# Linear attention and a gated feed-forward layer on one core: the late sums of g behind the fourth division, and the units of seven products in block 2 too

## The chip, the cores and the metric

One core of a Trainium2 chip runs the kernel. The metric is the device time of one execution in microseconds. Before the change it is 277.55 us, the median of three runs (277.35 to 277.58).

## The reference

The inputs are q, k and v of shape [8, 8, 576, 64] (batch, heads, positions, head width), w_in [512, 2048] and w_out [2048, 512], all float32. The first stage is linear attention with position weights, the second a feed-forward layer:

```
phi(x) = concat(relu(x) * cos_w, relu(x) * sin_w)      # features 64 -> 128, weights by position
kv  = sum over s of phi(k)[s, f] * v[s, d]             # per batch and head, 128 x 64
z   = sum over s of phi(k)[s, f]
x   = (phi(q) @ kv) / (phi(q) @ z + 1e-6)              # heads side by side: [4608, 512]
h   = x @ w_in
g   = h * sigmoid(1.702 * h)
out = g @ w_out                                        # [4608, 512] float32
```

## The kernel before

One block of work is one batch, 576 rows of x: four chunks of 128 rows and a chunk of 64. The 512 rows are multiplied with w_in and w_out in the block; the 64-row chunks of all batches are collected in `xt` and worked off in the last block. Matrix operands are bf16, sums float32 in PSUM.

**What a block does.** While block b is multiplied, the x of block nb = b + 1 is made. For nb, feature maps of k (`trig`, two VectorE instructions for each of nine column groups) go to `kr`; `kv_next` multiplies them with v (72 small matmuls at L237) and VectorE copies the result out (L245). Then `x_next(nb, c)` (L965) makes chunk c of x in three steps: `num_mm` (L304), eight matmuls of 65 columns into a PSUM tile of the pool `pat`; `num_div` (L315), three VectorE instructions (L321 adds 1e-6, L323 inverts, L325 multiplies and writes bf16); `xturn_dma` (L351), a transposing DMA from SP's queue into the tile xT. The pool `pat` has two tiles, so the numerator of chunk c + 2 waits for the division of chunk c.

**The product with w_out** uses Winograd's form of Strassen's scheme: seven products of half size in place of eight. They are called p1, p2, p6, p5, p7, p3, p4, in this order (L481), each in two halves of eight matmuls of 256 columns (`wino_mm`, L509). Steps s = 0 to 13 of the loop at L1021 are these fourteen halves. The operands that are sums of blocks of g are made by `g_sums` (L466) on VectorE, each in two halves h of 1024 columns: s1 and s2 (read by p5 and p6), s3 (read by p7) and s4 (read by p3). Results go from three PSUM banks through copies on ScalarE (`keep`, L528: p1, u2, p5) and sums on VectorE (`join`, L539) to `ysb`, and out by DMAs that GpSimd issues (L526).

**The product with w_in** has two forms. In the plain form (`mm1`, L373) it is sixteen column groups fc of four matmuls of 512 columns (L365), each followed by the gelu on ScalarE (L371). In the form with units (`mm1_pair`, L724) two objects of class `Unit` (L643) make eight of the sixteen groups with seven products of half size each (L658, 256 columns), and the other eight go the plain way (`mm1_at`, L718, into `pat`, and L768, L773). A unit needs sums of blocks of w_in (`win_sum`, L615, held in `ws_pair` inside the tile `gt`), sums of blocks of x (`x_pair`, L712, made at the end of the block before), three VectorE adds (L667) and three ScalarE copies (L672), for which seven slots in `gt` and in the three `kept` tiles serve in rotation (L708). Blocks in PAIR (L699), 3 to 6, take the form with units; blocks 0, 1 and 2 the plain one; block 7 takes another with four units.

**What sets the order.** The kernel is scheduled by hand: each engine works off its instructions in the order in which the program states them, and waits at each one for the semaphores of its operands. The loop at L971 states it for a block. In the wino loop, a step states its products, then the keep or join of the product that has ended, then `x_next` for the chunks in `at` (L1017), then a feature map of the block after next's q on ScalarE (`trig_q`, from step 4 on in blocks 3 to 5, from step 8 on in blocks 1 and 2) with its transposing DMA on SP (`qturn_dma`), and then `g_sums`. In blocks 3 to 6 `x_next` of chunk 0 stands ahead of step 0 and the others at steps 1, 3, 4 and 6 (in block 6 the chunks 4, 1, 2, 3); `g_sums` of s3 stand at step 1 and of s4 at step 5. Block 2 has the divisions at steps 1, 3, 5 and 7 and makes s3 and the first half of s4 earlier, at fc 12. SP's queue carries the loads of q, k and v and all transposes, in the order of the program: the load of v for the block after next behind chunk 3 (L1030), then chunk 4's transpose, the five of q, then in the next block the loads of q and k (L749, in `mm1_pair` behind the last feature map of k; L986 in the plain form).

**Block 0** is a start-up with its own order. VectorE's part of it that the change touches is L915 to L921: after the fifth division it makes the eighteen feature maps of block 1's k (from the load at L844), then the first sum of w_out's blocks (`w_sum_1`). The block of w_in that holds its last 1024 columns is loaded at L843. The sums of w_in for the units are made in block 2 (L992).

Of the kernel before, what the change touches and what calls it, by code (L numbers as in the profile page):

```python
# [20 lines left out]
def kernel(  # L21
# [9 lines left out]
    nc = tc.nc  # L31
    B, H, S, D = q.shape
# [24 lines left out]
    def src_of(src, b, i0=0, i1=NI):  # L57
        return src[b, 2 * i0:2 * i1].rearrange("(i hh) (p j) d -> (hh p) i (j d)", hh=2, j=NS)

    qf = one.tile([128, 2560], F32, name="qf")  # L60
    kf, vf = [one.tile([128, NI, S], F32, name=n) for n in ("kf", "vf")]
# [62 lines left out]
    def load(t, src, b, eng=nc.gpsimd):  # L124
        eng.dma_start(out=t, in_=src_of(src, b))
# [24 lines left out]
    def load_wout(g):  # L150
        nc.gpsimd.dma_start(out=w_out_sb[:, ts(g, 4), :], in_=wout_r[g])
# [9 lines left out]
    def trig(dst, src, j, act=False, eng=nc.vector):  # L161

        i = src[:, :, ts(j, 64)]
        for cs, w in enumerate((cosw, sinw)):
            o = dst[:, j, :, ts(cs, 64)]
            if act is True or (act == "sin" and cs == 1):
                nc.scalar.activation(o, i, AF.Relu, scale=w[:, j:j + 1])
            else:
                eng.tensor_scalar(o, i, 0.0, w[:, j:j + 1], op0=MAX, op1=MUL)  # L169
# [73 lines left out]
    def kv_evac(i0, i1, n=65):  # L243
        o = st["kvs"][:, :, i0:i1, 0:n]
        nc.vector.tensor_copy(o, st["ps", i0].rearrange("p hh (i e) -> p hh i e", e=n))  # L245
# [58 lines left out]
    def num_mm(c, eps_too=False):  # L304
        ps = pat.tile([128, 2, 512], F32, name="at")
        if eps_too:
            for a in range(2):
                put_eps(ps[:, a])
        for h in range(H):
            nc.tensor.matmul(ps[:, h // 4, ds((h % 4) * 65, 65)], qT[:, h, ts(c, 128)],  # L310
                             kvs_of(h), start=not eps_too,
                             stop=(not eps_too or h % 4 == 3), skip_group_check=eps_too)
        nums[c] = [ps]

    def num_div(c, eps_too=False):  # L315
        ps = nums[c][0]
        pv = ps[:, :, 0:260].rearrange("p a (h e) -> p a h e", h=4)
        den = pv[:, :, :, 64]
        if not eps_too:
            den = small.tile([128, 2, 4], F32, name="den")  # L320
            nc.vector.tensor_scalar(den, pv[:, :, :, 64], 1e-6, None, op0=ADD)  # L321
        inv = small.tile([128, 2, 4], F32, name="inv")
        nc.vector.reciprocal(inv, den)  # L323
        xn = small.tile([128, 2, 4, 64], BF16, name="xn", bufs=5)
        nc.vector.tensor_tensor(xn, pv[:, :, :, 0:64],  # L325
                                inv.unsqueeze(3).to_broadcast([128, 2, 4, 64]), op=MUL)
        nums[c].append(xn)
# [23 lines left out]
    def xturn_dma(b, c):  # L351
        xn = nums.pop(c)[1]
        n = 128 if c < 4 else 64
        nc.sync.dma_start_transpose(out=x_cols(b, c),
                                    in_=xn[0:n].rearrange("p a h e -> p (a h e)"))
# [110 lines left out]
    def g_sums(names, h, of=MAIN):  # L466

        tt = nc.vector.tensor_tensor
        a_blk, to = of
        o = {n: to[n][:, ts(h, 4)] for n in to}  # L470
        for n in names:
            if n == "s1":
                tt(o[n], a_blk(1, h), a_blk(1, h + 2), op=ADD)  # L473
            elif n == "s2":
                tt(o[n], o["s1"], a_blk(0, h), op=SUB)  # L475
            elif n == "s3":
                tt(o[n], a_blk(0, h), a_blk(1, h), op=SUB)  # L477
            else:
                tt(o[n], a_blk(0, h + 2), o["s2"], op=SUB)
# [135 lines left out]
    def win_sum(n, i, ws=ws):  # L615
        tt = nc.vector.tensor_tensor
        o = {m: ws[m][:, :, ts(i, 512)] for m in ws}
        a = {(0, k): w_in_t[i][:, ts(k, 2), :] for k in range(2)}
        a.update({(1, k): w_in_t[2][:, ts(k, 2), ts(i, 512)] for k in range(2)})
        if n == "s1":  # L620
            tt(o[n], a[1, 0], a[1, 1], op=ADD)
        elif n == "s2":
            tt(o[n], o["s1"], a[0, 0], op=SUB)
        elif n == "s3":
            tt(o[n], a[0, 0], a[1, 0], op=SUB)
        else:
            tt(o[n], a[0, 1], o["s2"], op=SUB)
# [15 lines left out]
    class Unit:  # L643
# [31 lines left out]
        def step(self, p):  # L675
# [17 lines left out]
            else:  # L693
# [2 lines left out]

    PAIR = range(3, B - 1)  # L699
    gt_flat = gt.rearrange("p f e -> p (f e)")  # L700
    ws_pair = {n: gt_flat[:, ts(i, 1024)].rearrange("p (k f) -> p k f", k=2)
               for i, n in enumerate(("s1", "s2", "s3", "s4"))}
# [86 lines left out]
    def kv_mm_next():  # L789
        kv_open()  # L790
        kv_mm(0, 4, vt_rhs, 0, 65)

    def kv_next():
        kv_mm_next()
        kv_evac(0, 4)
# [120 lines left out]
    load_wout(2)  # L916
    load(vf, v, 1)
    load_wout(3)
    for j in range(NS):
        trig(kr, kf, j)  # L920
    w_sum_1()  # L921
# [43 lines left out]
    def x_next(b, c):  # L965
        num_mm(c)
        num_div(c)
        xturn_dma(b, c)


    for b in range(1, B):  # L971
        nb = b + 1 if b + 1 < B else None
        if nb is None:
            break
        f0 = 5 if b == 1 else 0
        if b in PAIR:
            mm1_pair(b, nb)
        for fc in range(f0, FC) if b not in PAIR else ():
            if b == 1 and fc == f0:
                for c in range(5):  # L980
                    trig_q(c)
                    qturn_dma(c)
            if nb is not None and fc == f0 + 1:
                kv_operands(nb)

                if nb + 1 < B:  # L986
                    if b == 1:
                        load(kf, k, nb + 1, nc.sync)
                    load_q(nb + 1, nc.sync)
                    if b > 1:  # L990
                        load(kf, k, nb + 1, nc.sync)
                if b == 2:  # L992
                    for n in ws_pair:
                        win_sum(n, 0, ws_pair)
            if fc == 8 and b == 1:
                vcopy()
            if fc == 12:
                if b > 1:
                    g_sums(("s3",), 0)
                    g_sums(("s3",), 1)  # L1000
                g_sums(("s1", "s2", "s4") if b > 1 else ("s1", "s2"), 0)
            if fc == 14 and nb is not None and b > 1:
                kv_next()
            mm1(b, fc)
        if nb is not None:
            x_open(nb)
            if b == 2:
                x_next(nb, 0)
            if b == 1:
                kv_mm_next()  # L1010
            g_sums(("s1", "s2"), 1)
            if b > 2:
                x_next(nb, 0)
            if b == 1:
                kv_evac(0, 4)
                g_sums(("s3",), 0)
            at = ({2: [0], 3: [1], 4: [2], 6: [3], 8: [4]} if b == 1 else  # L1017
                  {2 * p + 1: [p + 1] for p in range(4)} if b == 2 else
                  {s: [p + 1 if nb < B - 1 else (4, 1, 2, 3)[p]] for p, s in enumerate((1, 3, 4, 6))})
            wino_open()  # L1020
            for p in range(7):  # L1021
                for c in range(2):
                    wino_mm(p, c)
                    s = 2 * p + c
                    if c == 1:
                        wino_after(b, p)
                    for c2 in at.get(s, ()):
                        x_next(nb, c2)
                        if c2 == 3 and nb + 1 < B:
                            load(vf, v, nb + 1, nc.sync)  # L1030

                    s0 = 4 if b > 2 else 8
                    if s0 <= s < s0 + 5 and nb + 1 < B:
                        trig_q(s - s0, act=True)
                    if 8 <= s < 13 and nb + 1 < B:
                        qturn_dma(s - 8)
                    if s == 1 and b == 2:
                        g_sums(("s4",), 1)
                    if s == 1 and b > 2:
                        g_sums(("s3",), 0)  # L1040
                        g_sums(("s3",), 1)
                    if s == 5 and b > 2:
                        g_sums(("s4",), 0)
                        g_sums(("s4",), 1)
                    if s == 2 and b == 1:
                        g_sums(("s3",), 1)
                    if s == 4 and b == 1:
                        g_sums(("s4",), 0)
                    if s == 6 and b == 1:
                        g_sums(("s4",), 1)  # L1050
            if nb in PAIR:
                x_pair(nb)
# [3 lines left out]
    b = B - 1  # L1056
# [103 lines left out]
```

## Time and profile before

| what | value |
|---|---|
| median of three runs | 277.55 us |
| the profiled execution | 277.53 us, span 275.6 us |
| TensorE (PE) busy | 267.9 us, 97% of the span |
| VectorE (DVE) busy | 203.0 us, 74% |
| ScalarE (ACT) busy | 172.8 us, 63% |
| GpSimd (POOL) busy | 43.0 us, 16% |
| blocks 2, 3, 4, 5, 6 by the chain of waits | 28.60, 28.50, 28.49, 28.48, 28.49 us |
| granted TensorE clock | 1.00 |
| HBM | 36.70 MB read, 9.44 MB written |

The span runs from the program's first instruction to its last; the execution's own time holds 1.9 us more around it. A group's busy time counts overlapping instructions once. A matmul's drawn length covers its way through the array, so matmuls that follow each other overlap in the record: what one costs is the distance of its start to the next start (0.109 us for 256 columns, 0.216 us for 512). VectorE's and ScalarE's instructions overlap a little in the same way: a product L325 is drawn 0.69 us long and the next instruction starts after 0.61. A bracket behind an instruction holds the idle time of its engine just before it and what ended it.

### The profile page before, as it was taken

To read this page: it belongs to the slowest core of one execution; us is meant where nothing else is said; L and a number is where in the kernel's file an instruction comes from. 1 tells how busy PE (TensorE), PEld (TensorE's weight loads), DVE (VectorE), ACT (ScalarE), POOL (GpSimd) and SP (SyncE) were. 2 spreads that over 40 slices of the span, in tenths; PEclk is the share of its full clock that TensorE was granted. 3 is DMA by queue.
4 is the path that set the end of the run, shared out by engine and by line. 5 is a ranking of instruction groups with operands and counts; after the bars stand their busy time and mean duration, and the time that the engine had idled before them with its cause. 6 is when DMAs were issued, how large, how long until landed. Compare 5 with 4: busy or idle time off the path is not lost.

```text
span 275.6 us, 6999 instructions
## 1 busy us (share of the span) xinstructions
PE 267.9 (97%) x2844; PEld 204.5 (74%) x2844; DVE 203.0 (74%) x476; ACT 172.8 (63%) x311; POOL 43.0 (16%) x71
## 2 busy tenths in 40 slices
PE   8899999999999999999999999999999999999994
PEld 2585645856975699778877887788778876999983
DVE  4943775698899596879887988888888985744741
ACT  6967642584297519974788387848683147677621
POOL 5691000000122012100210022001200163000310
PEclk9999999999999999999999999999999999999999
DMA  7999999999999897997799689999991754000233
GB/s 232 253 211 298 278 295 162 255 305 197 301 207 289 225 262 192 255 242 206 187 299 233 195 114 278 170 284 194 236 196 23 107 149 139 0 0 2 82 111 114
DMA packets 73663, 53.60 MB, mean 194 GB/s; under 512 B 52736, under 2 KB 63488, under 8 KB 73632
## 3 DMA queue, kind: packets, MB, share of 16 engines
q1 hardware_dynamic: 67504, 36.97, 60.9%
q0 software_dynamic: 6128, 16.19, 22.6%
q8 instruction: 22, 0.36, 0.6%
q14 instruction: 9, 0.07, 0.1%
HBM read 36.70 MB, written 9.44 MB: 167 GB/s over the span
## 4 chain that ended last, share of the span: by engine, by line
PE 81%; DVE 12%; DMA 4%; issue 1%; ACT 0%; POOL 0%
PE mm L520 22%; PE mm L365 16%; PE mm L658 14%; PE at L721 8%; PE mm L421 5%; PE at L520 4%; PE mm L396 4%; PE at L237 4%; DVE xn L325 3%; DMA sums<-in_v_dram 2%; DVE sums L475 2%; PE at L310 2%; DVE sums L477 2%; DVE sums L473 2%; DMA kf<-in_k_dram 1%; DVE inv L323 1%
## 5 line engine op out<-in xcount | busy, mean ns | idle before, releaser
L365 PE MATMUL mm<-xT,w_in 128*128 128x512 bf16 (+1 forms) x304 | 51.4, 320 | 0.0
L526 POOL DMA_DIRECT2D out_dram<-ysb x24 | 18.1, 754 | 182.0 <-DVE den L321 124.6
L520 PEld LDWEIGHTS <-sums 128*128 128x128 bf16 x448 | 42.5, 98 | 4.6
L371 ACT ACTIVATE g<-mm 128x512 bf16<-128x512 f32 x56 | 32.2, 597 | 14.6 <-PE mm L365 14.6
L365 PEld LDWEIGHTS <-w_in 128*128 128x128 bf16 x304 | 27.6, 114 | 17.3
L520 PE MATMUL mm<-wsum,sums 128*128 128x256 bf16 x336 | 39.9, 272 | 0.0
L520 PEld LDWEIGHTS <-g 128*128 128x128 bf16 x336 | 32.0, 98 | 3.6
L169 DVE TENSOR_SCALAR kr<-kf,cosw 128x256 bf16<-128x256 f32 x69 | 24.5, 355 | 5.3 <-DMA kf<-in_k_dram 5.3
L325 DVE TENSOR_TENSOR xn<-at,inv 128x512 bf16<-128x512 f32 x39 | 27.0, 691 | 1.3
L520 PE MATMUL mm<-w_out_sb,g 128*128 128x256 bf16 x224 | 26.6, 273 | 0.0
L169 DVE TENSOR_SCALAR kr<-kf,sinw 128x256 bf16<-128x256 f32 x68 | 23.5, 345 | 0.0
L721 PE MATMUL at<-xT,w_in 128*128 128x512 bf16 x96 | 23.3, 379 | 0.0
L183 ACT ACTIVATE qn<-qf,cosw 128x512 bf16<-128x512 f32 (+1 forms) x27 | 19.2, 712 | 2.2 <-DMA qf<-in_q_dram 2.2
L183 ACT ACTIVATE qn<-qf,sinw 128x512 bf16<-128x512 f32 (+1 forms) x27 | 19.2, 710 | 0.0
L535 ACT ACTIVATE kept_p<-mm 128x512 f32<-128x512 f32 (+1 forms) x15 | 8.5, 566 | 16.7 <-PE mm L520 14.9
L658 PE MATMUL mm<-xT,w_in 128*128 128x256 bf16 x128 | 18.6, 273 | 0.0
L658 PEld LDWEIGHTS <-w_in 128*128 128x128 bf16 x144 | 15.9, 113 | 2.7
L310 PEld LDWEIGHTS <-qT 128*128 128x128 bf16 x312 | 13.8, 97 | 5.1 <-issue 3.7
L658 PE MATMUL mm<-xT,gt 128*128 128x256 bf16 x128 | 17.2, 272 | 0.0
L310 PE MATMUL at<-kvs,qT 128*128 128x65 bf16 x312 | 15.7, 193 | 1.3 <-DVE den L321 1.3
L535 ACT ACTIVATE kept_u<-mm 128x512 f32<-128x512 f32 (+1 forms) x8 | 4.4, 544 | 18.8 <-PE mm L520 15.4
L658 PEld LDWEIGHTS <-gt 128*128 128x128 bf16 x128 | 14.1, 113 | 2.4 <-issue 0.9
(175 smaller groups left out, 452.6 us busy)
## 6 DMA issues: line engine op xcount, KB each, us to landing
kf<-in_k_dram SPq DMA_DIRECT2D x6, 1152.0 KB, 9.1
vf<-in_v_dram SPq DMA_DIRECT2D x6, 1152.0 KB, 7.0
qf<-in_q_dram SPq DMA_DIRECT2D x6, 1024.0 KB, 6.5
out_dram<-ysb POOLq DMA_DIRECT2D x24, 256.0 KB, 5.5
w_out_sb<-in_moe_w_out_dram POOLq DMA_DIRECT2D x4, 512.0 KB, 17.2
kf<-in_k_dram POOLq DMA_DIRECT2D x1, 1152.0 KB, 13.1
vf<-in_v_dram POOLq DMA_DIRECT2D x1, 1152.0 KB, 20.3
w_in<-in_moe_w_in_dram POOLq DMA_DIRECT2D x2, 512.0 KB, 10.0
```

Source lines behind the costliest of these rows:

```text
L169: eng.tensor_scalar(o, i, 0.0, w[:, j:j + 1], op0=MAX, op1=MUL)
L183: nc.scalar.activation(o, i, AF.Relu, scale=sc)
L310: nc.tensor.matmul(ps[:, h // 4, ds((h % 4) * 65, 65)], qT[:, h, ts(c, 128)], kvs_of(h), start=not eps_too, stop=(not eps_too or h % 4 == ...
L325: nc.vector.tensor_tensor(xn, pv[:, :, :, 0:64], inv.unsqueeze(3).to_broadcast([128, 2, 4, 64]), op=MUL)
L365: nc.tensor.matmul(hp[fc][:, t0:t1], wcol(kc, fc), x[b][:, kc, t0:t1], start=(kc == 0), stop=(kc == KC - 1))
L371: nc.scalar.activation(gT[fc // 4][:, fc % 4], hp.pop(fc), AF.Gelu_apprx_sigmoid)
L421: nc.tensor.matmul(yp[b, t, c0][:, c0:c1], w, w_out_sb[:, fc, c0:c1], start=(fc == 0), stop=(fc == FC - 1))
L520: nc.tensor.matmul(bank[to][c], lhs, rhs, start=opens, stop=(fc == HF - 1), skip_group_check=True)
L526: eng.dma_start(out=dst[:, 2 * i + c0:2 * i + c1, ts(n, HD)], in_=t[:, c0:c1])
L535: nc.scalar.activation(o, i, AF.Identity)
L658: nc.tensor.matmul(to[:, j], lhs, rhs, start=(opens and j == 0 and k == 0), stop=(k == 1), skip_group_check=True)
L721: nc.tensor.matmul(hp[fc], wcol(kc, fc), x[b][:, kc], start=(kc == 0), stop=(kc == KC - 1))
```

## The change

`PAIR` begins at block 2, so that block 2 takes the form with units as well (and `x_pair` for it runs at the end of block 1). The four sums of w_in's blocks that it needs are made in block 0, ahead of the feature maps of block 1's k. What block 2 did otherwise than blocks 3 to 6 in its own loop goes away: its divisions now stand at steps 1, 3, 4 and 6 too, and chunk 0's behind the second halves of s1 and s2; its feature maps of q stay at steps 8 to 12. In blocks 2 to 6 the four halves of s3 and s4 all stand at step 4, behind `x_next` of that step, which is the fourth division of the block.

```diff
-    PAIR = range(3, B - 1)
+    PAIR = range(2, B - 1)
...
     load(vf, v, 1)
     load_wout(3)
+    for n in ws_pair:
+        win_sum(n, 0, ws_pair)
     for j in range(NS):
         trig(kr, kf, j)
     w_sum_1()
...
                 if nb + 1 < B:
-                    if b == 1:
-                        load(kf, k, nb + 1, nc.sync)
+                    load(kf, k, nb + 1, nc.sync)
                     load_q(nb + 1, nc.sync)
-                    if b > 1:
-                        load(kf, k, nb + 1, nc.sync)
-                if b == 2:
-                    for n in ws_pair:
-                        win_sum(n, 0, ws_pair)
             if fc == 8 and b == 1:
                 vcopy()
             if fc == 12:
-                if b > 1:
-                    g_sums(("s3",), 0)
-                    g_sums(("s3",), 1)
-                g_sums(("s1", "s2", "s4") if b > 1 else ("s1", "s2"), 0)
-            if fc == 14 and nb is not None and b > 1:
-                kv_next()
+                g_sums(("s1", "s2"), 0)
             mm1(b, fc)
         if nb is not None:
             x_open(nb)
-            if b == 2:
-                x_next(nb, 0)
             if b == 1:
                 kv_mm_next()
             g_sums(("s1", "s2"), 1)
-            if b > 2:
+            if b > 1:
                 x_next(nb, 0)
...
             at = ({2: [0], 3: [1], 4: [2], 6: [3], 8: [4]} if b == 1 else
-                  {2 * p + 1: [p + 1] for p in range(4)} if b == 2 else
                   {s: [p + 1 if nb < B - 1 else (4, 1, 2, 3)[p]] for p, s in enumerate((1, 3, 4, 6))})
...
-                    if s == 1 and b == 2:
-                        g_sums(("s4",), 1)
-                    if s == 1 and b > 2:
-                        g_sums(("s3",), 0)
-                        g_sums(("s3",), 1)
-                    if s == 5 and b > 2:
-                        g_sums(("s4",), 0)
-                        g_sums(("s4",), 1)
+                    if s == 4 and b > 1:
+                        for n in ("s3", "s4"):
+                            g_sums((n,), 0)
+                            g_sums((n,), 1)
```

## The prediction

> **What bounds the kernel now.** I read the page's engine shares and its chain first, then the busy time of each engine over the blocks, then VectorE's and TensorE's instructions in order of time inside one block.
>
> ```profile
> PE 267.9 (97%) x2844; PEld 204.5 (74%) x2844; DVE 203.0 (74%) x476; ACT 172.8 (63%) x311; POOL 43.0 (16%) x71
> ...
> PE 81%; DVE 12%; DMA 4%; issue 1%; ACT 0%; POOL 0%
> ```
>
> TensorE is the bound, yet 12% of the chain that ends last is VectorE's. The chain shows where the blocks start, at 80.68, 109.28, 137.78, 166.27, 194.75 and 223.24 us. The windows between them are blocks 2 to 6; here blocks 2, 3 and 4 (columns: window, its length, busy us of PE, PEld, DVE, ACT, POOL, clock, DMA):
>
> ```profile
> 80.68:109.28 28.60, 28.60 (x291) 20.50 (x289) 21.58 (x50) 17.87 (x31) 3.61 (x5) 1.00 0.98 245
> 109.28:137.78 28.50, 28.18 (x315) 22.84 (x313) 24.04 (x58) 21.11 (x39) 2.91 (x5) 1.00 0.89 224
> 137.78:166.27 28.49, 28.17 (x314) 22.82 (x313) 24.03 (x58) 20.32 (x36) 2.90 (x5) 1.00 0.91 214
> ```
>
> Block 2 multiplies w_in in the plain way and never idles. Blocks 3 to 6 already use the two units of seven products, and save only 0.1 us by it: each has the same hole. In block 4 the chain goes through it:
>
> ```profile
> 156.69 1.28 DVE sums L477 x2
> 157.97 0.60 DVE ysb L545
> ...
> 158.91 0.69 DVE xn L325
> 159.61 0.08 DVE den L321
> 159.69 0.06 issue
> 159.75 0.40 PE at L310 x8
> ```
>
> The same place in VectorE's and TensorE's order of time:
>
> ```profile
> 156.08 0.69 DVE L325 TENSOR_TENSOR xn<-at,inv 128x512 bf16<-128x512 f32 x1
> 156.69 1.28 DVE L477 TENSOR_TENSOR sums<-g 128x1024 bf16<-128x1024 bf16 x2
> 157.89 0.68 DVE L545 TENSOR_TENSOR ysb<-mm,kept_p 128x512 f32<-128x512 f32 x1
> 158.49 0.16 DVE L321 TENSOR_SCALAR den<-at 128x8 f32<-128x8 f32 x1
> ...
> 159.52 0.16 DVE L321 TENSOR_SCALAR den<-at 128x8 f32<-128x8 f32 x1
> ...
> 160.56 1.28 DVE L479 TENSOR_TENSOR sums<-g,sums 128x1024 bf16<-128x1024 bf16 x2
> ```
>
> ```profile
> 157.53 1.91 PE L520 MATMUL mm<-wsum,sums 128*128 128x256 bf16 x16
> 159.75 0.40 PE L310 MATMUL at<-kvs,qT 128*128 128x65 bf16 x8 [0.32 <-DVE den L321]
> ```
>
> The fifth numerator (chunk 4, at 159.75) needs the PSUM tile of the third (chunk 2), which is free when the third division's product ends (158.91 + 0.69 = 159.60; then 0.15 to TensorE). That division stands behind the two s3 sums. How large is the hole? The sixteen matmuls issue every 0.109 us (157.53, 157.635, ..., 159.16), so the numerator could start at 159.27: 0.48 us. The bracket says 0.32, because the last matmul is drawn 0.27 long. The Trainium skill ("Perfetto Trace Analysis", Identifying the Most-Contended Engine) warns that matmul busy time is a poor measure because pipelined matmuls look different from what they cost; with 0.32 in the sum below it would end at 276.1. The spacing decides: 0.48.
>
> **The change part by part** (times of the profiled execution, 277.53 us with a span of 275.6; the median of the runs shown is 277.55, so one sum serves for both).
>
> 1. *Late sums, blocks 3 to 6.* New order on VectorE: divisions 1 and 2, the join of p1 and p2 (L545), divisions 3 and 4, s3 twice, s4 twice, division 5. Up to 156.69 nothing moves. Then: join 0.60 to 157.29; third division 1.03 (158.49 to 159.52) to 158.32, its product written at 158.40, plus 0.15 is 158.55. TensorE asks at 159.27, so the 0.48 goes, with 0.72 to spare. What is late next: fourth division to 159.35, s3 twice at 0.60 to 160.55, s4 twice to 161.75, fifth division to 162.78 (before: 162.80). The seventh product p7 reads s3. TensorE is there at 159.27 + 0.24 (numerator) + 0.87 (eight matmuls of p5) = 160.39 and needs the second half four matmuls later, 160.82; that half is written at 160.63 and reaches TensorE at 160.78. Cover 0.04 us, the thinnest of all. p3 reads s4: first matmul at 160.39 + 1.75 = 162.13, halves with TensorE at 161.38 and 161.98; the second is needed at 162.57. Free. The join of p7 then runs at 162.78 to 163.38 and p4 writes that bank at 163.88. Free.
>
>  p3 also writes the bank that ScalarE's copy of p5 reads:
>
> ```profile
> 160.93 0.71 ACT L183 ACTIVATE qn<-qf,sinw 128x512 bf16<-128x512 f32 x1
> 161.54 0.58 ACT L535 ACTIVATE kept_p<-mm 128x512 f32<-128x512 f32 x1
> ```
>
>  The copy queues behind four feature maps of q, does not move, and ends at 162.12; with the 0.15 to TensorE p3 starts at 162.27 at the latest instead of 162.13. Bounds: 0 (copy seen at once) to 0.14; I take 0.10. Block 6 has no feature maps of q, so nothing there. Gain: blocks 3, 4, 5 each 0.48 - 0.10 = 0.38, block 6 0.48; together **1.62**.
>
> 2. *Units in block 2.* Leaves: 64 matmuls of 512 columns at 0.216 = 13.82. Comes: 32 x 0.216 + 56 x 0.109 = 13.02, so 0.80 less TensorE work. What comes with it (six adds, six copies, four x sums, the waits of the units' banks) need not be priced singly: blocks 3 to 6 hold all of it. Block 2 becomes a block of 28.49 with the hole, 28.01 without: 28.60 - 28.01 = **0.59**. Its copy of p5 is ahead of its feature maps of q (they stay at steps 8 to 12), so the 0.10 does not arise. Late at its start: the x sums wait for the fourth chunk of block 2's x, whose DMA is issued at 76.27 and lands 4.25 later, 80.52. Four sums take 1.46 (108.18 to 109.64 in block 3), six feature maps of k 1.57: 83.55. The first add cannot start before block start + 3.31 (112.43 - 109.12) = 80.56 + 3.31 = 83.87. Covered by 0.3. ScalarE enters block 2 at 82.29 + 0.48, some 0.3 later against its start than in block 3; the first bank that this can hold up is the third regular product's, with about 0.1 to spare. Between 0 and 0.2 lost; I take 0, as in block 3. SP's loads of q and k stand behind five transposes until 91.35 in both kernels, and the k feature maps end before (88.5), so they do not move.
>
> 3. *w_in sums in block 0.* Four sums at 0.63 (86.26 to 88.79 for four) = 2.53 leave block 2 and come ahead of block 1's feature maps of k. VectorE idles there:
>
> ```profile
> 26.74 0.35 DVE L169 TENSOR_SCALAR kr<-kf,cosw 128x256 bf16<-128x256 f32 x1 [2.68 <-DMA kf<-in_k_dram]
> ```
>
>  It is free at 24.06, the last third of w_in lands at 12.81 + 11.1 = 23.91, and 24.06 + 2.53 = 26.59 is ahead of 26.74. Cost 0. Without that cover the feature maps slip, by at most 2.53, and a second idle time of 2.2 us (35.05, for q) takes it.
>
> Sum: 1.62 + 0.59 = 2.21. **277.53 - 2.21 = 275.3 us.** With p3's wait at 0 or 0.14, the units' start at 0 to 0.2: 275.0 to 275.6.
>
> **The rivals.**
>
> *The wait moves.* p7 has 0.04 of cover. If the four sums go at 0.69 each, as where one sum waits for another (L475), and not 0.60, s3's second half comes 0.18 later and p7 stalls 0.14 in five blocks: 276.0. For it: the cover is thin. Against: s3 and s4 read nothing that was just written, and ran at 0.60 in pairs.
>
> *The transfers do not follow.* The feature maps of q of block 5 start late, at 184.80, held 1.28 us by the load of q: 18.7 us after the block's start (166.10), against 14.9 for that load in block 4. ScalarE then needs 1.24 + 0.49 + 2.45 + 0.58 + 0.1 until p5's copy is done, so p3 (24.5 after the start) stalls from a landing at 19.6. If the transfers keep their old clock while TensorE gains 1.35 us by block 5, the load lands at 20.05: 0.4 lost, 275.8 with its neighbours. [...] Against: an earlier load also ends earlier.
>
> *Slower.* The same queue, further: between blocks 4 and 5 one slow stretch cost the load of q 3.8 us. A second such stretch ahead of block 5 would bring it at 18.7 + 0.4 + 3.8 = 22.9 and p3 would stall 3.3: 278.6. It decides from a landing 2.8 us past 19.6. Against: one stretch in four blocks, and the next load is issued only after the last.
>
> *The sums' move does nothing*, since the numerator waits for something else than the third product. Then block 2 alone counts, 28.60 to 28.49: 277.4. Against: the wait ends 0.15 after that product in all four blocks.
>
> **How the numbers follow.** Forecast 0.62 (275.0 to 275.6), the moved wait 0.15 (276.0), transfers 0.10 (275.8), nothing moved 0.07 (277.4), slower 0.06 (278.6). The range 274.8 to 276.6 holds the first three with a margin for their bounds. A measurement of this kernel tells 0.2%, 0.55 us, from no change: faster 0.87, same 0.07, slower 0.06.
>
> **What would show it.** Blocks 2 to 6 about 28.0 to 28.1 long; no idle time ahead of the fifth numerator; VectorE's four sums in a row, ending near block start + 24.1; p3's first matmul behind the copy of p5 by 0.1 in blocks 3 to 5; the w_in sums between 24.06 and 26.7 with the feature maps of k starting where they did. Wrong would be a new gap ahead of p7, a block 2 longer than its fellows, or ScalarE waiting for q in blocks 4 and 5 by several us.

## The result, and the profile after

The changed kernel takes **275.37 us** (median of 6 runs, 275.05 to 276.1) against 277.52 for the kernel before (6 runs beside it): a ratio of 0.9926, 95% interval 0.9913 to 0.994. It is faster by 2.15 us; the forecast was 275.3. Executions in which TensorE's granted clock was lowered are left out of all figures: there were three, all of the changed kernel in a second set (mean clock 0.85, 0.85 and 0.56; 309, 309 and 461 us).

The page of the changed kernel; its profiled execution took 275.49 us around a span of 273.4:

```profile
PE 265.7 (97%) x2847; PEld 207.2 (76%) x2868; DVE 207.8 (76%) x487; ACT 174.8 (64%) x317; POOL 42.4 (15%) x71
...
PE 93%; DMA 4%; DVE 1%; issue 1%; ACT 0%; POOL 0%
```

VectorE has more to do than before (207.8 us instead of 203.0) and is hardly on the chain any more: its part of it falls from 12% to 1%, TensorE's rises from 81% to 93%. An engine's share of busy time says nothing about whether it is waited for. Blocks 2, 3, 5 and 6 of the changed kernel (block 4 has 28.05; columns: window, its length, busy us of PE, PEld, DVE, ACT, POOL, clock, DMA):

```profile
80.82:108.84 28.02, 27.86 (x311) 22.92 (x313) 24.91 (x60) 20.00 (x37) 2.90 (x5) 1.00 1.00 247
108.84:136.88 28.04, 27.88 (x311) 22.88 (x313) 23.95 (x58) 21.20 (x39) 2.90 (x5) 1.00 1.04 245
...
164.93:193.04 28.11, 27.95 (x312) 22.90 (x313) 23.96 (x58) 20.31 (x36) 2.91 (x5) 1.00 0.93 224
193.04:221.06 28.02, 27.86 (x311) 22.84 (x312) 24.03 (x57) 14.31 (x26) 2.93 (x5) 1.00 0.61 131
```

The lengths were 28.60, 28.50, 28.49, 28.48 and 28.49: the five blocks give back 0.58, 0.46, 0.44, 0.37 and 0.47, together 2.32. TensorE's busy time stays a little under the length, and the count of its matmuls under 315, because some records are missing, not because it idles. The profiled executions differ by only 2.04 (277.53 to 275.49). The other 0.28 lies outside these blocks: block 2 begins 0.14 later (80.82 instead of 80.68), because the first load of k landed 3.90 us behind its issue instead of 3.76; the time around the span is 0.16 longer; and what follows block 6 is 0.02 shorter.

The place of the hole in block 4, on VectorE:

```profile
156.82 0.69 DVE L325 TENSOR_TENSOR xn<-at,inv 128x512 bf16<-128x512 f32 x1
...
158.47 1.28 DVE L477 TENSOR_TENSOR sums<-g 128x1024 bf16<-128x1024 bf16 x2
159.67 1.29 DVE L479 TENSOR_TENSOR sums<-g,sums 128x1024 bf16<-128x1024 bf16 x2
```

and on TensorE:

```profile
156.63 1.91 PE L520 MATMUL mm<-wsum,sums 128*128 128x256 bf16 x16
158.38 0.41 PE L310 MATMUL at<-kvs,qT 128*128 128x65 bf16 x8
158.62 2.78 PE L520 MATMUL mm<-wsum,sums 128*128 128x256 bf16 x24
161.28 1.91 PE L520 MATMUL mm<-w_out_sb,sums 128*128 128x256 bf16 x16
```

The product of the third division is now with TensorE 0.7 us ahead of the fifth numerator (156.82 + 0.69 = 157.51, plus 0.15 to TensorE; the numerator starts at 158.38), and there is no bracket behind the numerator: 156.63 + 16 x 0.109 = 158.37 is where the matmuls before it end. The four sums follow in one row behind the fourth division. s3 ends at 159.75; with the 0.15 that the prediction reckoned it is with TensorE at 159.90. p7, eight matmuls into the group of 24, needs its second half at 158.62 + 12 x 0.109 = 159.93. By this reckoning 0.03 us of cover is left there; the run with s4 first, below, shows that it is more. p3 begins at 161.28 instead of 158.62 + 24 x 0.109 = 161.24, 0.05 behind the end of ScalarE's copy of p5:

```profile
160.65 0.58 ACT L535 ACTIVATE kept_p<-mm 128x512 f32<-128x512 f32 x1
```

### The profile page after: what moved, and what is told of

Its sections match the earlier page's. It is cut to its first block, busy times and chain, and to the rows that moved or that the text cites. A ratio compares the mean times of both kernels' runs of the same rounds, so it can differ in the third digit from the quotient of the medians.

```text
span 273.4 us, 7042 instructions
## 1 busy us (share of the span) xinstructions
PE 265.7 (97%) x2847; PEld 207.2 (76%) x2868; DVE 207.8 (76%) x487; ACT 174.8 (64%) x317; POOL 42.4 (15%) x71
## 4 chain that ended last, share of the span: by engine, by line
PE 93%; DMA 4%; DVE 1%; issue 1%; ACT 0%; POOL 0%
PE mm L520 31%; PE mm L658 16%; PE mm L365 13%; PE at L721 9%; PE mm L421 5%; PE at L520 4%; PE mm L396 4%; PE at L237 4%; PE at L310 3%; DMA sums<-in_v_dram 2%; DMA kf<-in_k_dram 1%; PE at L342 1%; PE mm L389 1%; DVE xn L325 1%; PE mm L205 0%
## 5 line engine op out<-in xcount | busy, mean ns | idle before, releaser
L526 POOL DMA_DIRECT2D out_dram<-ysb x24 | 17.4, 727 | 180.2 <-DVE inv L323 88.2
L365 PE MATMUL mm<-xT,w_in 128*128 128x512 bf16 (+1 forms) x239 | 38.7, 305 | 0.5
L371 ACT ACTIVATE g<-mm 128x512 bf16<-128x512 f32 x42 | 24.1, 598 | 10.9 <-PE mm L365 10.9
L365 PEld LDWEIGHTS <-w_in 128*128 128x128 bf16 x248 | 21.3, 114 | 11.5
L721 PE MATMUL at<-xT,w_in 128*128 128x512 bf16 x110 | 27.8, 379 | 0.5
L658 PE MATMUL mm<-xT,w_in 128*128 128x256 bf16 x152 | 22.0, 273 | 0.0
L658 PE MATMUL mm<-xT,gt 128*128 128x256 bf16 x160 | 21.5, 272 | 0.0
L658 PEld LDWEIGHTS <-w_in 128*128 128x128 bf16 x168 | 18.6, 114 | 3.3
L183 ACT ACTIVATE qn<-qf,cosw 128x512 bf16<-128x512 f32 (+1 forms) x27 | 19.2, 711 | 1.5 <-DMA qf<-in_q_dram 1.1
L658 PEld LDWEIGHTS <-gt 128*128 128x128 bf16 x160 | 17.6, 113 | 3.0 <-issue 1.2
L721 PEld LDWEIGHTS <-w_in 128*128 128x128 bf16 x120 | 13.5, 113 | 8.2
L183 ACT ACTIVATE qn<-qf,sinw 128x512 bf16<-128x512 f32 (+1 forms) x27 | 19.2, 709 | 0.0
L371 ACT ACTIVATE g<-at 128x512 bf16<-128x512 f32 x30 | 17.5, 598 | 2.0 <-PE at L721 1.3
## 6 DMA issues: line engine op xcount, KB each, us to landing
vf<-in_v_dram POOLq DMA_DIRECT2D x1, 1152.0 KB, 20.8
```

The lines of the kernel that those rows point to most:

```text
L183: nc.scalar.activation(o, i, AF.Relu, scale=sc)
L365: nc.tensor.matmul(hp[fc][:, t0:t1], wcol(kc, fc), x[b][:, kc, t0:t1], start=(kc == 0), stop=(kc == KC - 1))
L371: nc.scalar.activation(gT[fc // 4][:, fc % 4], hp.pop(fc), AF.Gelu_apprx_sigmoid)
L526: eng.dma_start(out=dst[:, 2 * i + c0:2 * i + c1, ts(n, HD)], in_=t[:, c0:c1])
L658: nc.tensor.matmul(to[:, j], lhs, rhs, start=(opens and j == 0 and k == 0), stop=(k == 1), skip_group_check=True)
L721: nc.tensor.matmul(hp[fc], wcol(kc, fc), x[b][:, kc], start=(kc == 0), stop=(kc == KC - 1))
```

## The experiments

The theory: the gain comes from VectorE's order. The third division stood behind sums that nobody wanted yet; with it ahead, the hole closes, and block 2's seven products can show what they save. The rivals: the units in block 2 bring the gain by themselves; the place behind the fourth division matters, and not only the third; and, for what remains, the loads of q, which ScalarE waits for ahead of its copy of p5, set how long a block takes. Each ratio is against the kernel before, run in turn on the same chip (277.40 to 277.45).

**The late sums alone** (block 2 stays plain):

```diff
-                    if s == 1 and b > 2:
-                        g_sums(("s3",), 0)
-                        g_sums(("s3",), 1)
-                    if s == 5 and b > 2:
-                        g_sums(("s4",), 0)
-                        g_sums(("s4",), 1)
+                    if s == 4 and b > 2:
+                        for n in ("s3", "s4"):
+                            g_sums((n,), 0)
+                            g_sums((n,), 1)
```

> Only the four late sums move in blocks 3 to 6; block 2 stays plain. My theory: the hole of 0.48 us in each of the four blocks goes, less what p3 waits for the copy of p5 (0.04 to 0.10 by the profile of the changed kernel): blocks 3 to 6 at 28.02 to 28.11 us, block 2 at 28.60, time 277.5 - 1.75 = 275.8 (ratio 0.9937). Rival, the gain comes from the units in block 2 and the hole closes only together with them: 277.5. Rival, the two parts lean on each other through the transfers: somewhere between, with a block longer than 28.2.

275.85 us (275.54 to 276.65), ratio 0.9945 (0.9933 to 0.9956). Its blocks 2 and 3:

```profile
80.42:108.99 28.57, 28.57 (x291) 20.51 (x289) 21.59 (x50) 17.57 (x31) 4.05 (x5) 1.00 1.02 241
108.99:137.09 28.10, 28.10 (x314) 22.87 (x313) 23.94 (x58) 21.10 (x39) 2.89 (x5) 1.00 0.91 228
```

Block 2 stays at 28.57, and block 3 loses the hole (block 4 too, at 28.05). This is the term of 1.62: the median is 1.58 under the kernel before.

**The units in block 2 alone** (the changed kernel, with the sums at steps 1 and 5 as before, in block 2 too):

```diff
-                    if s == 4 and b > 1:
-                        for n in ("s3", "s4"):
-                            g_sums((n,), 0)
-                            g_sums((n,), 1)
+                    if s == 1 and b > 1:
+                        g_sums(("s3",), 0)
+                        g_sums(("s3",), 1)
+                    if s == 5 and b > 1:
+                        g_sums(("s4",), 0)
+                        g_sums(("s4",), 1)
```

> Only block 2 takes the form with units, with its sums of w_in in block 0; the late sums stay where the blocks with units had them before, s3 at step 1 and s4 at step 5, in block 2 too. My theory: block 2 becomes a block with the same hole, 28.49 us instead of 28.60, and blocks 3 to 6 stay at 28.49; time 277.4 (ratio 0.9996, not to be told from none). Rival, the units are worth their 0.80 us of TensorE work whatever VectorE does: 276.7. Rival, the extra VectorE work in block 0 or at the start of block 2 costs: above 277.7.

277.42 us (277.28 to 278.57), ratio 1.0003 (0.9994 to 1.0012): nothing. Block 2, and in TensorE's order of time its fifth numerator:

```profile
80.42:108.92 28.50, 28.17 (x314) 22.81 (x313) 24.80 (x60) 19.80 (x37) 2.89 (x5) 1.00 1.07 245
```

```profile
102.41 0.40 PE L310 MATMUL at<-kvs,qT 128*128 128x65 bf16 x8 [0.33 <-DVE den L321]
```

The block has less to multiply and idles for most of the difference, in the hole that the other four have. Alone, the late sums are worth about 1.6 us and the units 0.1 in block 2, which the whole time does not show; together they are worth 2.15: the units' saving shows only where the hole is closed.

**The sums one division earlier, behind the third:**

```diff
-                    if s == 4 and b > 1:
+                    if s == 3 and b > 1:
```

> As changed, but the four sums stand at step 3, behind the third division and ahead of the fourth. My theory: the fifth numerator needs the third product alone, so the hole stays closed, and p7 gains 1.03 us of cover; the fourth division comes 2.4 us later and nothing on TensorE asks for it before the next block: time as changed, 275.4 (within 0.3). Rival, it is the fourth division that had to come first (its product or its transpose is what is late next): above 276.0, with a hole ahead of the fifth numerator or at the next block's start. If the thin cover of p7 cost something in the changed kernel, this one is faster by it.

275.13 us (275.04 to 275.89), ratio 0.9922 (0.991 to 0.9935), not to be told from the changed kernel. VectorE in block 4:

```profile
156.78 0.69 DVE L325 TENSOR_TENSOR xn<-at,inv 128x512 bf16<-128x512 f32 x1
157.39 1.28 DVE L477 TENSOR_TENSOR sums<-g 128x1024 bf16<-128x1024 bf16 x2
```

What must stand ahead of the sums is the third division. The bracket in the kernel before names L321, the first instruction of the fourth; here the fifth numerator starts at 158.34, ahead of that instruction (159.79), and the hole stays closed. s3 starts 1.04 us earlier in the block, and since nobody waited for it, that brings nothing. It only widens p7's cover.

The place has a price that the time does not show yet. The fourth division comes later, and with it its transpose on SP's queue (issued at 160.95 in block 4, in the changed kernel at 159.47) and the loads behind it. SP issues the load of q 12.1 to 13.0 us behind the first matmuls of blocks 3, 4 and 5, instead of 8.3 to 10.0, and q lands 18.4 to 19.2 behind them, instead of 14.7 to 16.9: close to the 19.6 from which the prediction let p3 stall. That the whole delay comes from the later transpose is likely and not shown.

**The cover of p7 taken away** (s4 made first, s3 last):

```diff
-                        for n in ("s3", "s4"):
+                        for n in ("s4", "s3"):
```

> As changed, but with the two halves of s4 ahead of those of s3, so that s3 comes 1.20 us later. This tests the cover of p7 (0.04 us for the second half by the sum, 0.03 in the profile of the changed kernel). My theory: the first half reaches TensorE at 1.0 us past p7's start and the second 0.17 later than its own use: p7 stalls 1.16 us in each of the five blocks, time 275.4 + 5.8 = 281.2. Rival, p7 has more cover than the sum says (TensorE asks later, or the sums go faster): below 280. If the fifth numerator waited for the sums and not for the third product, the hole would not come back here either, so this run does not tell that apart.

280.55 us (280.48 and 280.61), ratio 1.0112 (1.0094 to 1.013): slower than the kernel before. TensorE at p7 of block 3:

```profile
133.22 2.09 PE L520 MATMUL mm<-wsum,sums 128*128 128x256 bf16 x16 [0.75 <-DVE sums L477]
```

VectorE there, where L477 makes s3:

```profile
132.48 1.29 DVE L477 TENSOR_TENSOR sums<-g 128x1024 bf16<-128x1024 bf16 x2
```

By the spacing of the matmuls p7 loses 0.92 us ahead of its first half and 0.15 ahead of its second, 1.07 in a block. In block 4 it is 0.36 and 0.15, because TensorE comes there 0.56 late, after a pause inside p6 that no wait in the trace explains. The 1.16 worked out for a block was 0.09 too much, since it reckoned with 0.15 from VectorE to TensorE: the two halves of s3 are written at 133.16 and 133.76, and the matmuls that read them start at 133.22 and 133.82, 0.06 later. So s3 has little to spare in the changed kernel, but more than 0.03: ready at 159.75 + 0.06 = 159.81 for a use at 159.93 it has 0.12, and 1.20 us later costs 1.07, which leaves 0.13.

**Twice the w_in sums in block 0** (four more VectorE sums, which repeat the first four):

```diff
-    for n in ws_pair:
+    for n in (*ws_pair, *ws_pair):
         win_sum(n, 0, ws_pair)
```

> As changed, but the four sums of w_in are made twice in block 0 (the same values written again), 2.5 us more of VectorE ahead of the feature maps of block 1's k. My theory: the first set fills the wait for k's load; the second pushes the feature maps by about 2.2 us, from 27.2 to 29.4, and the next wait of 2.4 us (for q's load) takes it up: the same time, 275.4 within 0.3. Rival, work ahead of those feature maps is on the path: 277.6.

275.24 us (275.2 to 275.47), ratio 0.9922 (0.991 to 0.9935): no cost. VectorE in block 0 of the changed kernel,

```profile
27.21 0.35 DVE L169 TENSOR_SCALAR kr<-kf,cosw 128x256 bf16<-128x256 f32 x1 [0.34 <-DMA kf<-in_k_dram]
...
35.69 0.48 DVE L185 TENSOR_SCALAR qn<-qf,cosw 128x512 bf16<-128x512 f32 x1 [2.39 <-DMA qf<-in_q_dram]
```

and with the sums made twice:

```profile
28.85 0.35 DVE L169 TENSOR_SCALAR kr<-kf,cosw 128x256 bf16<-128x256 f32 x1
...
35.20 0.49 DVE L185 TENSOR_SCALAR qn<-qf,cosw 128x512 bf16<-128x512 f32 x1 [0.40 <-DMA qf<-in_q_dram]
```

The four sums end at 26.80 and take the time in which VectorE waits for k; the next four push the feature maps of k 1.6 us back (2.2 were expected), and the second wait, for q, shrinks by 2.0 in their place.

**The load of q behind the load of k**, to bring the transfer rival about:

```diff
         if nb + 1 < B:
-            load_q(nb + 1, nc.sync)
             load(kf, k, nb + 1, nc.sync)
+            load_q(nb + 1, nc.sync)
```

> As changed, but in the blocks with units SP issues the load of k ahead of that of q, so that q lands later while all else stays. This tests the price that I gave to a late load of q: p3 stalls from a landing at 19.7 us after the block's start, one for one. In the changed kernel it lands at 16.9, 14.7 and 16.1 us in blocks 3, 4 and 5. Behind k's 1.15 MB it should land at about 21.5, 19.8 and 20.5: stalls 1.9, 0.1 and 0.9, time 278.2 (between 277.2 and 279). Rival, the queue of ScalarE has slack that I did not see, or TensorE does not wait for the copy of p5: 275.4.

275.81 us, ratio 0.9953 (0.993 to 0.9977): the expected 278.2 was missed, but the ten runs lie between 275.11 and 278.93, where no other kernel here spreads by more than 1.5. In the profiled run, one of the shortest (275.23), q landed at 127.63, 155.16 and 183.16, which is 18.7 to 19.2 us behind the first matmuls of blocks 3, 4 and 5 (at 108.40 in block 3) and just under the 19.6 that the prediction worked out. ScalarE waited there (1.25 us in block 5), TensorE waited no more than in the changed kernel (0.04, 0.04 and 0.10 ahead of p3): blocks 3, 4 and 5 took 28.05, 28.05 and 28.11.

In the changed kernel q landed at 125.55, 151.44 and 180.90, 14.7 to 16.9 behind them. The run of 278.93 has no trace. That q came past the threshold there is likely by the next kernel, and not shown.

**Work put into TensorE's waits** (the sums at step 3, the first numerator of each block behind the first half of p1, and the 72 small matmuls of `kv_next` split by a gelu's product):

```diff
+        kv_open()
+        kv_mm(0, 1, vt_rhs, 0, 65)
         V.step(3)
         gelu(14)
-        kv_next()
+        kv_mm(1, 4, vt_rhs, 0, 65)
+        kv_evac(0, 4)
...
-            if b > 1:
-                x_next(nb, 0)
...
-                  {s: [p + 1 if nb < B - 1 else (4, 1, 2, 3)[p]] for p, s in enumerate((1, 3, 4, 6))})
+                  {s: [p if nb < B - 1 else (0, 4, 1, 2, 3)[p]] for p, s in enumerate((0, 1, 3, 4, 6))})
...
-                    if s == 4 and b > 1:
+                    if s == 3 and b > 1:
```

> The four sums behind the third division, and two of the small waits that are left in each of blocks 2 to 6 filled with other TensorE work: the first quarter of the k-v products goes ahead of the second unit's third product (which waits 0.13 us for an add), and the first numerator goes behind the first half of p1 (it waits 0.07 us for the copy of the k-v products). My theory: VectorE's order has the slack for it once the sums stand behind the third division, and each block loses 0.20 to 0.25 us: time 275.3 - 1.1 = 274.2. Rival, VectorE's gapless run from the k-v copy on is what sets the pace, and what TensorE gains at its start it waits for at the third or fourth numerator: 275.2.

276.26 us (275.43 to 276.93), ratio 0.995 (0.9932 to 0.9969): missed: the median is 0.9 above the changed kernel's, though the two intervals still overlap. The profiled execution (276.42) shows two reasons. The split of `kv_next` costs 0.10 us a block instead of saving some (last section). And the load of q came late in block 3, which took 29.09 us (block 4 28.09). Its window, and ScalarE's and TensorE's order of time in it:

```profile
108.39:137.48 29.09, 28.21 (x314) 22.93 (x313) 23.23 (x55) 21.38 (x39) 2.90 (x5) 1.00 1.19 226
```

```profile
129.20 0.72 ACT L183 ACTIVATE qn<-qf,cosw 128x512 bf16<-128x512 f32 x1 [3.34 <-DMA qf<-in_q_dram]
...
133.37 0.57 ACT L535 ACTIVATE kept_p<-mm 128x512 f32<-128x512 f32 x1
```

```profile
133.99 1.91 PE L520 MATMUL mm<-w_out_sb,sums 128*128 128x256 bf16 x16 [0.88 <-ACT kept_p L535]
```

This is the transfer rival, caught in a trace. ScalarE waits 3.34 us for q, the copy of p5 stands behind its feature maps, and p3 waits for the copy: 1.04 us by the spacing of the matmuls, 0.88 by the bracket. The feature maps began 20.8 us behind the block's first matmul (129.20 - 108.39), so the wait begins at 20.8 - 1.04 = 19.8; the prediction had 19.6. This kernel has its sums at step 3 too, and SP issued that load 13.0 us behind the block's start.

**The feature maps of q from step 8 on**, behind the copy of p5, in all blocks:

```diff
-                    s0 = 4 if b > 2 else 8
+                    s0 = 8
```

> As changed, but ScalarE makes the feature maps of q from step 8 on in blocks 3 to 5 too, behind the copy of p5. My theory: what is left of p3's wait (0.04, 0.04 and 0.10 us) goes, 0.18 in all; but ScalarE then enters blocks 4 to 6 some 1.6 us late, as it enters block 3, which so far cost between 0 and 0.17 us in a block's first products. Time 275.2 to 275.7, not to be told from the changed kernel. Rival, the wait of p3 is worth more than its gap, since it is where late loads of q show: below 275.0 and with less spread between runs.

275.04 us (274.86 to 275.38), ratio 0.9915 (0.9903 to 0.9927): just under the expected 275.2 to 275.7, just short of the rival's 275.0, and not to be told from the changed kernel. Block 5 of it, 28.11 in the changed kernel:

```profile
164.47:192.49 28.02, 28.02 (x315) 22.90 (x313) 23.96 (x58) 19.82 (x37) 2.91 (x5) 1.00 0.94 231
```

p3's wait is gone in all blocks, blocks 4 to 6 lose nothing at their start, and the five runs lie within 0.52 us.

**Both: k first, and the feature maps from step 8 on** (the two edits above together):

> The load of k ahead of that of q, as in the run whose times spread from 275.1 to 278.9, and the feature maps of q from step 8 on, behind the copy of p5. My theory: the late load of q costs only through ScalarE's queue ahead of that copy; with the copy ahead the same late loads cost nothing: 275.1 with a spread under 0.6. Rival, the later load of q slows something else (its transposes, or the next block's start): above 275.5, or the spread stays.

275.00 us (274.91 to 275.36), ratio 0.9912 (0.9899 to 0.9925). q landed as late as with k first alone (128.12, 155.49, 184.08), and the runs lie within 0.45 us (four runs) instead of 3.8 (ten). In block 3 the copy of p5 starts at 131.44, as soon as p5 is there, and the first feature map of q behind it at 131.93.

This speaks for the theory: the late load costs time by way of ScalarE's order. With so few runs the spread alone does not prove it. A trace shows it in the last kernel below: q lands 20.0 us behind block 3's first matmul, past the 19.8, and with the copy ahead the block takes 27.95.

Not every loss is q's. In the profiled execution here block 4 took 28.30, 0.29 more than blocks 3 and 5: TensorE paused inside the first half of p6, whose eight matmuls are drawn 1.32 us long (at 155.22) instead of 1.04, while ScalarE waited for TensorE. No wait in the trace ends there, and the cause stays open.

**The changed kernel again**, for its spread:

> The changed kernel itself, once more beside the others: 275.4 us. The runs of it lay between 275.05 and 276.1. If that spread is p3 waiting now and then for the copy of p5 behind a late load of q, it shows again here and not in the two kernels beside it.

275.06, 275.36 and 275.39 us, ratio 0.9919 (0.9905 to 0.9934). Three runs say nothing of a spread, so the question stays open; with the first six it is 275.05 to 276.1.

**The parts that held, together** (the sums at step 3, the first numerator behind the first half of p1, feature maps of q from step 8; `kv_next` left whole):

```diff
-            if b > 1:
-                x_next(nb, 0)
...
-                  {s: [p + 1 if nb < B - 1 else (4, 1, 2, 3)[p]] for p, s in enumerate((1, 3, 4, 6))})
+                  {s: [p if nb < B - 1 else (0, 4, 1, 2, 3)[p]] for p, s in enumerate((0, 1, 3, 4, 6))})
...
-                    s0 = 4 if b > 2 else 8
+                    s0 = 8
...
-                    if s == 4 and b > 1:
+                    if s == 3 and b > 1:
```

> The four sums behind the third division, the feature maps of q from step 8 on, and the first numerator behind the first half of p1. My theory: no wait of p3, cover of about a microsecond for p7, and 0.07 us less in each of blocks 2 to 6 (the wait for the copy of the k-v products): blocks of 27.95, time 274.7. Rival, the first division then comes too late for the third numerator: 275.1 or more.

274.89 us (274.55 to 275.05), ratio 0.9903 (0.9889 to 0.9917), the fastest kernel here. Its interval overlaps with the changed kernel's; the blocks show the gain:

```profile
80.38:108.60 28.22, 28.05 (x312) 22.99 (x313) 24.94 (x60) 20.27 (x38) 2.90 (x5) 1.00 0.96 232
108.60:136.55 27.95, 27.79 (x312) 22.96 (x313) 23.29 (x56) 19.76 (x37) 2.90 (x5) 1.00 1.11 224
```

Block 3 is 0.09 under that of the changed kernel, and block 4 is 27.96, again 0.09 under. Block 2 has 0.27 more than block 3: the first unit's third product waits 0.18 for ScalarE's copy (L672) out of its bank, and the next two 0.04 and 0.05, since ScalarE comes late out of block 1. That hangs on the load of q in block 1. Where it landed 4.39 us or more ahead of block 2's first matmul, as in the changed kernel and five others, block 2 lost nothing there; at 4.32 (`kv_next` split) it lost 0.05, at 4.22 (sums behind the third division) 0.17, and at 4.10 (this kernel) and 4.12 (s4 first) 0.27.

## Why the prediction was right, point by point

1. *The late sums, 1.62.* Blocks 3 to 6 gave 0.46, 0.44, 0.37 and 0.47, together 1.74. The mechanism is shown by the two parts run alone and by the sums behind the third division. The hole was worth its 0.48 by issue spacing, and not the 0.32 of the bracket: four times 0.32 would have been 1.28 at most. The Trainium skill ("Perfetto Trace Analysis", Identifying the Most-Contended Engine) calls matmul busy time a poor measure of how close a kernel is to roofline, because pipelined matmuls look smaller in the trace. That does not say how to size one wait, and here a matmul is drawn longer (0.27) than it costs (0.109).
2. *p3 behind the copy of p5, 0.10 in three blocks.* This term was too large: 0.04, 0.04 and 0.10 in blocks 3, 4 and 5. TensorE starts 0.05 us behind the end of ScalarE's copy (189.34 to 189.39 in block 5), where the prediction used the 0.15 from VectorE as its bound. Three times 0.10 were charged and 0.18 came, and this 0.12, less 0.01 of block 2, is what the blocks gained beyond the forecast.
3. *p7's cover, 0.04.* It held: no block stalls there, and the rival "the wait moves" did not happen. The size was wrong on the safe side. The 0.15 from VectorE to TensorE was read from the numerator; s3 reaches p7 in 0.06, as the kernel with s4 first shows, and the cover was 0.12 to 0.13.
4. *Units in block 2, 0.59.* Measured 0.58. The bound of 0 to 0.2 for its start came out at 0 in the changed kernel. Three other kernels lost 0.17 to 0.27 there, more than the bound, and the first bank that ScalarE held up was the first unit's, not the third regular product's.
5. *w_in sums in block 0, 0.* The cost was right, the times were not: the sums ended at 26.80 instead of 26.59, and k landed at 27.18, where it had landed at 26.72 before. Had it landed there again, the feature maps would have slipped by about 0.1, which the wait for q takes up, as the run with twice the sums shows.
6. *The transfers, and the slower case.* The mechanism is real, with a threshold of 19.8 against the 19.6 worked out. In the changed kernel's profiled execution the loads came early, 14.7 to 16.9 us behind the block's start. The expectation that k first would push q to 19.8 or later was wrong for the profiled run: q came 18.7 to 19.2 behind the start. The Trainium skill ("DMA: Bandwidth & Descriptors", Issuing engines are not separate DMA queues) says that all issuers share the same 16 engines; no run here tests that with q and k, since SP issues both.

In all, 2.32 in the blocks against 2.21, less the 0.28 outside them, which no step had foreseen. The mechanism was right; that the time came within 0.1 of the forecast is in part luck, since the two misses have opposite signs.

## What to carry to other kernels

A saving on the engine that is the bound shows only where that engine isn't waiting anyway: first close the hole, and look for it in the order of another engine's instructions, however low that engine's busy share. In a queue that works in order, put what frees a buffer ahead of what is wanted later, and work out the slack of the one moved back (here 0.12 us were enough, and 1.2 us less cost 1.07 a block). Ask also what the queues behind that engine issue later by the move. Work that waits for a load stands behind the copies that others wait for, since a load's landing varies, here by 2.2 us between three blocks of one execution.

## What the runs showed of the hardware

Going from the large matmuls with 128 rows to the small ones with 64 and back costs TensorE time that no wait explains. In the kernel that splits `kv_next`, at block 3:

```profile
120.25 0.45 PE L237 MATMUL at<-vt,kr 64*128 64x65 bf16 x18
120.63 0.63 PE L658 MATMUL mm<-xT,gt 128*128 128x256 bf16 x4
121.19 0.99 PE L237 MATMUL at<-vt,kr 64*128 64x65 bf16 x54
122.11 0.63 PE L365 MATMUL mm<-xT,w_in 128*128 128x512 bf16 x2
```

By the spacing of the starts, going in costs 0.10 us (0.205 from the last large matmul to the first small one, where 0.109 is usual), and coming out another 0.10 and 0.03 on the first large one, each time and with no bracket. The numerators, as narrow (65 columns) but with 128 rows, show no such cost. So the rows are the likely cause; no run here separates them from all else.

The split pays this change twice. The 18 and 54 small matmuls take 0.38 and 0.92 us up to the next large one, where the 72 in one piece take 1.19 in the changed kernel (121.11 to 122.30); the four large ones between them take 0.56 (120.63 to 121.19) instead of 4 x 0.109 = 0.44. That is 0.23 more, for a pause of 0.13 that it fills: the products behind L237 start 13.72 us behind the block's start instead of 13.62. Against the last kernel, which leaves `kv_next` whole, block 4 is 0.14 longer (28.10 against 27.96), 0.04 of it p3's wait.

The load of q, in the same place of SP's queue, landed between 13.8 and some 20.5 us behind the first matmuls of blocks 3, 4 and 5 in the kernels that issue it ahead of k. Most of that is when SP issued it, 7.9 to 13.3 us behind them; from issue to landing it took 5.6 to 7.6.
